# Batches 1 to 3 in chunks of 502 columns, and raw rows loaded by halves

## The chip, the cores and the metric

The kernel runs on one core of one Trainium2 chip. The metric is the device time of one execution in microseconds, from a median of runs. Engines: TensorE (PE, with its weight loads as PEld), VectorE (DVE), ScalarE (ACT), GpSimd (POOL) and SyncE (SP), which here only issues DMAs.

## The reference

```python
X = np.fft.fft(x, axis=1)              # x: (4, 3008, 256) f32, along 3008
X = np.fft.fft(X, axis=2)              # along 256
x = X.real.reshape(4 * 3008, 256)
h = x @ w_in                           # w_in: (256, 2048)
g = h * (1.0 / (1.0 + np.exp(-h)))
out = g @ w_out                        # w_out: (2048, 256)
```

## The kernel before

**The mathematics.** The transform along 256 is folded into w_in once, at the start (abh and abl, the high and low fp32r parts of the folded weights, and the row a128). The transform along 3008 is real-valued work on folded rows: sums and differences of four quarter-shifted and mirrored rows, then a product with cosine tables. By symmetry only 1506 columns of a batch are needed; each gives two outputs (signs + and -). They fall into four classes, CLASS, by the residue of the frequency: 376, 378, 376 and 376 columns. A class needs sums (sm) or rotated differences (ri) of the raw rows; operand(c) makes its operand xf from them, splits it into xh and xl, and transform(c) multiplies it with the tables into a PSUM pair. spread(c) turns that into uvh and uvl (high and low part, fp32r, ScalarE line 375 and VectorE line 378) and copies one row, which a DMA from SP (line 377) repeats on 128 partitions as ub.

**The main loop.** A chunk is one class of one batch: 16 chunks of 376 or 378 columns. Each has NF = 16 steps f, one for every 128 of the 2048 hidden columns. A step has four parts. first(c, f): 6 matmuls (lines 400 to 402, high x high, high x low, low x high, for two halves) into a pq pair in PSUM, of which there are two. act(c, f): VectorE adds ub times a128 (line 414) and makes sum and difference h (lines 418, 419), ScalarE applies Silu (430) and copies to gh (431). rest: VectorE makes gl = h - gh (441), one step later in its order. second(c, f): 12 matmuls (lines 458, 459, 465) into four accumulators in PSUM, LAG = 3 steps later. In chunk 0 twelve steps use f32 weights without the split (line 456), while w_out is converted. After f = 15 ScalarE copies the four accumulators to o tiles (473), four buffers shared with the row of spread, and SP writes them out (474).

**The order.** All is written out by hand. In the loop over steps come first(step), second(step - 3), at f = 12 the transform of the next class, act, rest(step - 1), spread of the transformed class, and then what plan holds for the step, and a few pieces of two queues: queue (operands, weight splits) with a budget of 0.6 a step and pool_queue (GpSimd's folds) with 0.6, in chunk 1 1.3. Each engine runs its own instructions in that order and waits on semaphores for the others.

**The folds.** load_x brings 4 x 2 x 256 raw values on 128 partitions (two buffers of 8 KB a partition), add_x adds the mirrored rows by an accumulating DMA from GpSimd's queue. fold_sums makes the sums and keeps the even-odd differences (od), fold_diffs reuses the same raw tile and od for the differences; ScalarE scales with the rotation (lines 254, 255) and GpSimd adds (259).

Of the kernel before, what the change touches and what calls it, by code (L numbers as in the profile page):

```python
# [50 lines left out]
def fft_mlp(ctx, tc, x1, x2, w_in, w_out, te, to, t2, t2f, rot1, rot2, dft, eye, out):  # L51
# [9 lines left out]
    cp = ctx.enter_context(tc.tile_pool(name="cp", bufs=2))  # L61
# [160 lines left out]
    def fold_diffs(k, i, ps=every):  # L222

        tt = nc.gpsimd.tensor_tensor
        g, od, rot = raw_x.pop((k, i))[ps], folded.pop(("od", k, i), None), rot_sb[k][ps]
        for h in range(2):
            if k + i == 0:
                tt(g[:, h, 0:2], g[:, h, 0:2], g[:, h, 2:4], op=ALU.subtract)
                yield 1.2
                keep = fold_p.tile([128, 2, 128], F32, tag="half", name="keep", bufs=3)[:, :, 1:]  # L230
                for j in range(2):
                    e, o = g[:, h, j, 1:128], g[:, h, j, 129:]
                    tt(keep[:, 1 - j], *((e, o) if j else (o, e)), op=ALU.subtract)
                yield 0.6
                tt(g[:, h, 0:2, 1:128], g[:, h, 0:2, 1:128], g[:, h, 0:2, 129:], op=ALU.add)
                nc.scalar.activation(g[:, h, 0:2, 129:], keep, AF.Copy)
                yield 0.6
                continue
            tt(g[:, h, 0:2, 0:129], g[:, h, 0:2, 0:129], g[:, h, 2:4, 0:129], op=ALU.subtract)
            yield 0.4  # L240
            if od:
                tt(g[:, h, 0, 129:], od[h][:, 1, 1:], od[h][:, 3, 1:], op=ALU.subtract)
                tt(g[:, h, 1, 129:], od[h][:, 2, 1:], od[h][:, 0, 1:], op=ALU.subtract)
            else:
                keep = fold_p.tile([128, 128], F32, tag="half", name="keep", bufs=3)[ps, 1:]
                tt(keep, g[:, h, 1, 129:], g[:, h, 3, 129:], op=ALU.subtract)
                tt(g[:, h, 1, 129:], g[:, h, 2, 129:], g[:, h, 0, 129:], op=ALU.subtract)
                nc.scalar.activation(g[:, h, 0, 129:], keep, AF.Copy)
            yield 0.6
        yield 0.6  # L250
        ri = fold_tile("ri", k, i, 2 - k)[ps]
        for h in range(2):
# [545 lines left out]
```

## Time and profile before

| | |
|---|---|
| time, median of 3 runs | 903.4 us (903.19 to 903.96) |
| profiled execution, span of its instructions | 901.8 us |
| TensorE busy | 881.9 us, 98%, 4982 matmuls |
| VectorE, ScalarE, GpSimd busy | 82%, 58%, 20% |
| chain that ended last | TensorE 92%, VectorE 4%, DMA 2% |

No time of its own is given for the profiled execution beside its span, so its own time is the span. Busy time counts the records of an engine; a matmul's record is longer than the time to the next one, since matmuls are pipelined, so starts and not durations tell TensorE's pace. In a row of the order of time the columns are start and length in us, engine, line, operation, out<-in, shapes and the number of merged instructions; a bracket holds the idle time before and what ended it.

### The profile page before, as it was taken

Reading aid. Unit: us, or ns where it says so; the run is one execution under the profiler, and the core shown is the slowest. Engines: PE = TensorE matmul, PEld = TensorE weight load, DVE = VectorE, ACT = ScalarE, POOL = GpSimd, SP = SyncE. Lnnn points to the kernel's source line nnn. Section 1 sums busy time; section 2 is a strip of 40 time slices with the busy share of each in tenths; the row PEclk is TensorE's granted clock in tenths of the full one; section 3 lists DMA queues with packets and bytes.
Section 4 is the critical chain, followed back from the end, with each engine's and each line's share of the span. In section 5 each row is a group of like instructions: output and inputs, shape, how many; then the busy total and the mean of one; then the engine's idle time right before and its main releaser. Section 6 shows DMA issues by size and latency. Waiting matters only on the chain.

```text
span 901.8 us, 12782 instructions
## 1 busy us (share of the span) xinstructions
PE 881.9 (98%) x4982; PEld 858.9 (95%) x4982; DVE 743.9 (82%) x1209; ACT 525.8 (58%) x728; POOL 179.4 (20%) x213
## 2 busy tenths in 40 slices
PE   6889999999999999999999999999999999999998
PEld 4567999999999999999999999999999999999998
DVE  6888888978889797987879698887879878786885
ACT  3625675646667564755746475665645656565554
POOL 1114051660123061460301025110100101010000
PEclk9999999999999999999999999999999999999999
DMA  9790315312030460203021060212103021210301
GB/s 297 159 300 8 44 24 79 82 5 39 1 29 17 71 159 4 41 1 25 20 10 35 3 134 1 10 35 9 35 2 42 1 9 35 9 35 1 44 1 35
DMA packets 19597, 42.65 MB, mean 47 GB/s; under 512 B 2464, under 2 KB 12704, under 8 KB 17616
## 3 DMA queue, kind: packets, MB, share of 16 engines
q1 hardware_dynamic: 17904, 31.87, 18.9%
q0 software_dynamic: 1632, 9.96, 5.5%
q8 instruction: 39, 0.64, 0.3%
q14 instruction: 22, 0.18, 0.1%
HBM read 26.39 MB, written 12.34 MB: 43 GB/s over the span
## 4 chain that ended last, share of the span: by engine, by line
PE 92%; DVE 4%; DMA 2%; issue 1%; ACT 1%; SPq 0%; DVEq 0%; ACTq 0%
PE acc L459 19%; PE acc L465 19%; PE acc L458 19%; PE pq L400 9%; PE pq L401 9%; PE pq L402 9%; PE pq L345 5%; DMA wo<-in_w_out_dram 1%; DMA win<-in_w_in_dram 1%; PE acc L456 1%; PE pq L210 1%; DVE wf L83 1%; PE pw L523 0%; DVE wf L85 0%; DVE wf L79 0%
## 5 line engine op out<-in xcount | busy, mean ns | idle before, releaser
L430 ACT ACTIVATE h<-h 128x752 f32<-128x752 f32 (+2 forms) x246 | 204.0, 829 | 284.3 <-DVE h L419 281.7
L459 PE MATMUL acc<-gh,wol 128*128 128x376 f32 (+1 forms) x976 | 326.8, 335 | 0.0
L458 PE MATMUL acc<-gh,woh 128*128 128x376 f32 (+1 forms) x976 | 326.3, 334 | 0.0
L441 DVE TENSOR_TENSOR gl<-h,gh 128x752 fp32r<-128x752 f32 (+2 forms) x246 | 242.0, 984 | 1.9 <-ACT gh L431 1.8
L465 PE MATMUL acc<-gl,woh 128*128 128x376 f32 (+1 forms) x976 | 216.1, 335 | 0.0
L431 ACT ACTIVATE gh<-h 128x752 fp32r<-128x752 f32 (+2 forms) x246 | 204.2, 830 | 7.8
L414 DVE SCALAR_TENSOR_TENSOR h<-ub,a,pq 128x376 f32<-128x376 f32 (+1 forms) x254 | 153.5, 604 | 58.3 <-PE pq L402 56.2
L459 PEld LDWEIGHTS acc<-gh,wol 128*128 128x128 f32 x976 | 183.7, 188 | 0.0
L458 PEld LDWEIGHTS acc<-gh,woh 128*128 128x128 f32 x976 | 183.5, 188 | 0.0
L400 PE MATMUL pq<-uvh,abh 128*128 128x376 f32 (+1 forms) x508 | 173.7, 342 | 2.8 <-DVE h L419 2.8
L465 PEld LDWEIGHTS acc<-gl,woh 128*128 128x128 f32 x976 | 172.8, 189 | 0.0
L401 PE MATMUL pq<-uvl,abh 128*128 128x376 f32 (+1 forms) x508 | 170.4, 335 | 0.0
L402 PE MATMUL pq<-uvh,abl 128*128 128x376 f32 (+1 forms) x508 | 170.2, 335 | 0.0
L419 DVE TENSOR_TENSOR h<-h,pq 128x376 f32<-128x376 f32 (+1 forms) x254 | 139.0, 547 | 8.7
L418 DVE TENSOR_TENSOR h<-h,pq 128x376 f32<-128x376 f32 (+1 forms) x254 | 138.9, 547 | 8.5
L320 POOL TENSOR_TENSOR xl<-xf,xh 128x256 fp32r<-128x256 f32 x53 | 49.6, 964 | 399.6 <-DVE h L419 244.6
L400 PEld LDWEIGHTS pq<-uvh,abh 128*128 128x128 f32 x508 | 95.6, 188 | 5.3 <-DVE h L419 4.0
L401 PEld LDWEIGHTS pq<-uvl,abh 128*128 128x128 f32 x508 | 95.9, 189 | 1.1
L402 PEld LDWEIGHTS pq<-uvh,abl 128*128 128x128 f32 x508 | 96.0, 189 | 0.0
L378 DVE TENSOR_TENSOR uvl<-pq,uvh 128x752 fp32r<-128x752 f32 (+1 forms) x16 | 15.1, 943 | 56.1 <-ACT row L376 56.1
L259 POOL TENSOR_TENSOR ri<-ri,raw 128x256 f32<-128x256 f32 (+1 forms) x28 | 27.5, 994 | 106.6 <-ACT ri L255 106.3
L456 PE MATMUL acc<-g,wof 128*128 128x376 f32 x96 | 33.5, 492 | 0.0
(117 smaller groups left out, 515.2 us busy)
## 6 DMA issues: line engine op xcount, KB each, us to landing
out_dram<-o SPq DMA_DIRECT2D x48, 188.0 KB, 2.3
raw<-in_x_dram SPq DMA_DIRECT2D x5, 1024.0 KB, 11.1
raw<-in_x_dram POOLq DMA_DIRECT2D x5, 1024.0 KB, 8.5
win<-in_w_in_dram SPq DMA_DIRECT2D x8, 512.0 KB, 9.4
wo<-in_w_out_dram SPq DMA_DIRECT2D x8, 512.0 KB, 9.9
out_dram<-o SPq DMA_DIRECT2D x16, 189.0 KB, 2.4
ub<-row SPq DMA_DIRECT2D x11, 188.0 KB, 8.7
te<-in_te_dram POOLq DMA_DIRECT2D x1, 1128.0 KB, 13.2
```

The lines of the kernel that those rows point to most:

```text
L400: nc.tensor.matmul(po, abh[:, i, fs], uvh[:, i, :n], start=True, stop=False)
L401: nc.tensor.matmul(po, abh[:, i, fs], uvl[:, i, :n], start=False, stop=False)
L402: nc.tensor.matmul(po, abl[:, i, fs], uvh[:, i, :n], start=False, stop=True)
L414: stt(p[:, :n], ub[:, :n], a128[f // 2][:, f % 2:f % 2 + 1], pq[:, 0, :n], op0=ALU.mult, op1=ALU.add)
L418: tt(h[:, 0, :n], p[:, :n], pq[:, 1, :n], op=ALU.add)
L419: tt(h[:, 1, :n], p[:, :n], pq[:, 1, :n], op=ALU.subtract)
L430: nc.scalar.activation(h[:, sg, :n], h[:, sg, :n], AF.Silu)
L431: nc.scalar.activation(gh[:, sg, :n], h[:, sg, :n], AF.Copy)
L441: tt(gl[:, sg, :n], g[:, sg, :n], gh[:, sg, :n].bitcast(F32), op=ALU.subtract)
L458: nc.tensor.matmul(po, wo[0][f // 2][:, f % 2, es], gh[:, sg, :n], start=f == 0, stop=False)
L459: nc.tensor.matmul(po, wo[1][f // 2][:, f % 2, es], gh[:, sg, :n], start=False, stop=False)
L465: nc.tensor.matmul(accs[c][i][:, :n], wo[0][f // 2][:, f % 2, es], gl[:, sg, :n], start=False, stop=f == NF - 1)
```

## The change

Batch 0 keeps four chunks, the class with k = 0 now first in the column order. The 4518 columns of batches 1 to 3 are cut into nine chunks of 502, without regard to classes, so a class can give columns to two chunks; spread writes each piece into its chunk. turns says at which step each class is transformed, begins when its operand is started. A raw tile now holds one half, and is loaded twice: for the sums and again for the differences, so od is gone, and both folds follow one plan (load, add 4 or 5 steps later, fold 3 steps after that). pool_queue's budget is 1.3 everywhere. h has two buffers instead of three, o three instead of four, uv and ub three. w_out's raw tiles use other buffers, the constants of the start share one tile with uv, and z is made in place in sm.

```diff
-CLASS = ((378, 376), (0, 378), (754, 376), (1130, 376))
-CH = 378
+CLASS = ((0, 376), (376, 378), (754, 376), (1130, 376))
+CH = 502
+CHUNKS = [n for _, n in CLASS] + [CH] * (3 * (B - 1))
+STARTS = [sum(CHUNKS[:j]) for j in range(len(CHUNKS))]
+LAST = len(CHUNKS) - 1
 LAG = 3
 FULL = 12
 DIRECT = 2
-PIECES = ((slice(0, 4),), (slice(0, 2), slice(2, 4)))
...
     def load_x(k, i, ps=every):
-        t = raw_x[k, i] = raws.tile([128, 2, 4, D], F32, tag="raw", name="raw")
-        nc.sync.dma_start(out=t[ps], in_=(x1, x2)[k][i, ps, 0])
+        for h in range(2):
+            t = raw_x[k, i, h] = raws.tile([128, 4, D], F32, tag="raw", name="raw")
+            nc.sync.dma_start(out=t[ps], in_=(x1, x2)[k][i, ps, 0, h])
 
     def add_x(k, i, ps=every):
 
-        nc.gpsimd.dma_start(out=raw_x[k, i][ps], in_=(x1, x2)[k][i, ps, 1], accum_op=ALU.add)
-
-    def fold_tile(name, k, i, bufs=1):
+        for h in range(2):
+            nc.gpsimd.dma_start(out=raw_x[k, i, h][ps], in_=(x1, x2)[k][i, ps, 1, h], accum_op=ALU.add)
...
-        g = raw_x[k, i][ps]
-        if k == 0:
-            od = fold_p.tile([128, 2, 4, 128], F32, tag="od", name="od")
-            od = [od[ps, h] for h in range(2)]
-        else:
-            od = [fold_p.tile([128, 4, 128], F32, tag="half", name="od", bufs=3)[ps] for h in range(2)]
-        folded["od", k, i] = od
         sm = fold_tile("sm", k, i)[ps]
         for h in range(2):
-            for js in PIECES[k]:
-                tt(od[h][:, js, 1:], g[:, h, js, 1:128], g[:, h, js, 129:], op=ALU.subtract)
-                yield 0.6
-                tt(g[:, h, js, 1:128], g[:, h, js, 1:128], g[:, h, js, 129:], op=ALU.add)
-                yield 0.6
-            tt(sm[:, h, :, 0:129], g[:, h, 0:2, 0:129], g[:, h, 2:4, 0:129], op=ALU.add)
+            g = raw_x.pop((k, i, h))[ps]
+            tt(g[:, 0:2], g[:, 0:2], g[:, 2:4], op=ALU.add)
+            yield 0.6
+            tt(sm[:, h, :, 1:128], g[:, 0:2, 1:128], g[:, 0:2, 129:], op=ALU.add)
             yield 0.4
-            tt(sm[:, h, :, 129:], od[h][:, 0:2, 1:], od[h][:, 2:4, 1:], op=ALU.add)
+            tt(sm[:, h, :, 129:], g[:, 0:2, 1:128], g[:, 0:2, 129:], op=ALU.subtract)
+            nc.scalar.activation(sm[:, h, :, ends], g[:, 0:2, ends], AF.Copy)
             yield 0.4
-
-    def first_sums(k, ps=every):
-
-        g = raw_x[k, 0][ps]
+        ready.add(("sm", k, i, ps.stop))
...
+    def chunk(j):
+        if j not in chunks:
+            uv = cp.tile([128, 2, 2, 512], F32R, tag="uv", name="uv")
+            chunks[j] = uv[:, 0], uv[:, 1], cp.tile([128, 512], F32, tag="ub", name="ub"), CHUNKS[j], STARTS[j]
+        return chunks[j]
+
     def spread(c, po):
 
-        uvh = cp.tile([128, 2, CH], F32R, tag="uvh", name="uvh")
-        uvl = cp.tile([128, 2, CH], F32R, tag="uvl", name="uvl")
-        ub = cp.tile([128, CH], F32, tag="ub", name="ub")
         b, k = divmod(c, 4)
         o, n = CLASS[k]
         o += b * NC
-        row = mp.tile([1, CH], F32, tag="o", name="row", bufs=4)
-        nc.scalar.activation(uvh[:, :, :n], po[:, :, :n], AF.Copy)
-        nc.scalar.activation(row[:, :n], po[0:1, 1, :n], AF.Copy)
-        (nc.sync if c else nc.gpsimd).dma_start(out=ub[:, :n], in_=row[:, :n].unsqueeze(0).to_broadcast([1, 128, n]))
-        tt(uvl[:, :, :n], po[:, :, :n], uvh[:, :, :n].bitcast(F32), op=ALU.subtract)
-        chunks[c] = uvh, uvl, ub, n, o
+        parts = []
+        for j, (at, m) in enumerate(zip(STARTS, CHUNKS)):
+            lo, hi = max(o, at), min(o + n, at + m)
+            if lo < hi:
+                uvh, uvl, ub, _, _ = chunk(j)
+                src, dst = slice(lo - o, hi - o), slice(lo - at, hi - at)
+                parts.append((uvh[:, :, dst], uvl[:, :, dst], ub[:, dst], src))
+        for uvh, _, _, src in parts:
+            nc.scalar.activation(uvh, po[:, :, src], AF.Copy)
+        for _, _, ub, src in parts:
+            row = mp.tile([1, CH], F32, tag="o", name="row", bufs=3)[:, :src.stop - src.start]
+            nc.scalar.activation(row, po[0:1, 1, src], AF.Copy)
+            (nc.sync if c else nc.gpsimd).dma_start(
+                out=ub, in_=row.unsqueeze(0).to_broadcast([1, 128, src.stop - src.start]))
+        for uvh, uvl, _, src in parts:
+            tt(uvl, po[:, :, src], uvh.bitcast(F32), op=ALU.subtract)
...
-            h = mp.tile([128, 2, CH], F32, tag="h", name="h", bufs=3)
+            h = mp.tile([128, 2, CH], F32, tag="h", name="h")
...
-                t = mp.tile([128, CH], F32, tag="o", name="o", bufs=4)
+                t = mp.tile([128, CH], F32, tag="o", name="o", bufs=3)
...
+    turns, begins = {}, {1: (0, 3), 2: (1, 9), 3: (2, 0), 4: (3, 2), 5: (3, 7), 6: (4, 0)}
+    for c in range(1, 4):
+        turns[c - 1, 12 + 2 * (c == 2)] = c
+    for b in range(1, B):
+        j, c = 3 * b + 1, 4 * b
+        for k, when in enumerate(((j - 1, 0 if b > 1 else 7), (j - 1, 12 if b > 1 else 14), (j, 8), (j + 1, 4))):
+            turns[when] = c + k
+            begins.setdefault(c + k + 1, when)
+        begins[c + 4], begins[c + 6] = (j + 1, 8), (j + 3, 3)
+    for c in range(1, 4 * B):
+        at(*begins[c], add, queue, ("op", c), operand(c))
...
+    def fold(name, k, i, j, f, *ps):
+        at(j, f, load_x, k, i, *ps)
+        at(j, f + 5 - (j < 3), add_x, k, i, *ps)
+        at(j, f + 8 - (j < 3), add, pool_queue, (name, k, i), {"sm": fold_sums, "ri": fold_diffs}[name](k, i, *ps))
+
+    at(0, 9, add, pool_queue, ("ri", 0, 0), fold_diffs(0, 0))
+    fold("ri", 1, 0, 0, 13)
+    fold("sm", 0, 1, 1, 9)
+    fold("sm", 1, 0, 2, 5, up)
+    fold("ri", 0, 1, 3, 1)
     for b in range(1, B - 1):
-        c = 4 * b + 1
-        at(c - 1, 14, load_x, 0, b + 1)
-        at(c, 0, add_x, 0, b + 1)
-        at(c, 4, add, pool_queue, ("t1", b + 1), fold_sums(0, b + 1))
-        at(c, 4, add, pool_queue, ("t1d", b + 1), fold_diffs(0, b + 1))
+        j = 3 * b + 1
+        fold("sm", 0, b + 1, j, 0)
+        fold("ri", 0, b + 1, j + 1, 6)
         if b % 2:
-            at(c - 1, 14, load_x, 1, b // 2 + 1)
-            at(c, 1, add_x, 1, b // 2 + 1)
-            at(c, 5, add, pool_queue, ("t2", b), fold_sums(1, b // 2 + 1))
-            at(c + 1, 5, add, pool_queue, ("t2d", b), fold_diffs(1, b // 2 + 1))
+            fold("sm", 1, b // 2 + 1, j, 11)
+            fold("ri", 1, b // 2 + 1, j + 2, 5)
...
-            if f == 12 and c + 1 < 4 * B:
+            turn = turns.get((c, f)) if n < len(steps) else None
+            if turn:
+                drain(queue, upto=("op", turn))
+                drain(pool_queue, upto=("x", turn))
                 new = pq_tile()
-                transform(c + 1, new)
+                transform(turn, new)
...
-            drain(pool_queue, 1.3 if c == 1 else 0.6)
+            drain(pool_queue, 1.3)
```

The new fold_diffs, which is not in this cut:

```python
def fold_diffs(k, i):
    tt = nc.gpsimd.tensor_tensor
    rot = rot_sb[k]
    for h in range(2):
        g = raw_x.pop((k, i, h))
        tt(g[:, 0:2], g[:, 0:2], g[:, 2:4], op=ALU.subtract)
        yield 0.6
        even, odd = g[:, 0:2, 1:128], g[:, 0:2, 129:]
        tt(g[:, 2:4, 1:128], even, odd, op=ALU.add)
        nc.scalar.activation(g[:, 2:4, ends], g[:, 0:2, ends], AF.Copy)
        yield 0.4
        tt(g[:, 2, 129:], even[:, 1], odd[:, 1], op=ALU.subtract)
        tt(g[:, 3, 129:], odd[:, 0], even[:, 0], op=ALU.subtract)
        yield 0.4
        ri = fold_tile("ri", k, i)
        for j in range(2):
            nc.scalar.activation(g[:, j], g[:, 3], AF.Copy, scale=rot[:, h, 1 - j:2 - j])
            nc.scalar.activation(ri[:, h, j], g[:, 2], AF.Copy, scale=rot[:, h, j:j + 1])
            yield 0.3
        for j, op in ((0, ALU.subtract), (1, ALU.add)):
            tt(ri[:, h, j], ri[:, h, j], g[:, j], op=op)
            yield 0.4
```

## Rows read from the trace of the kernel before

**Rows 1.** Busy time over the span: us, share, instructions.

```profile
PE 881.9 (98%) x4982; PEld 858.9 (95%) x4982; DVE 743.9 (82%) x1209; ACT 525.8 (58%) x728; POOL 179.4 (20%) x213
```

**Rows 2.** Waits of TensorE: us in total, times, longest.

```profile
PE pq L400 <- DVE h L419: 2.8, 2, 2.5
PE pq L334 <- DVE xf L272: 2.5, 1, 2.5
```

**Rows 3.** Stretch: PE, PEld, DVE, ACT, POOL busy, clock, DMA share, GB/s.

```profile
107.00:896.00 789.00, 789.00 (x4598) 789.00 (x4597) 658.53 (x1054) 474.45 (x643) 159.23 (x176) 1.00 0.20 31
```

**Rows 4.** Order of time on TensorE: one row a step, chunks 5 and 6.

```profile
323.93 0.85 PE L465 MATMUL acc<-gl,woh 128*128 128x378 f32 x4
...
352.05 0.85 PE L465 MATMUL acc<-gl,woh 128*128 128x378 f32 x4
...
376.97 0.85 PE L465 MATMUL acc<-gl,woh 128*128 128x376 f32 x4
...
401.84 0.85 PE L465 MATMUL acc<-gl,woh 128*128 128x376 f32 x4
```

**Rows 5.** Order of time on TensorE, f32 matmuls of the start.

```profile
16.37 3.60 PE L210 MATMUL pq<-raw,eye_sb 128*128 128x512 f32 x8
19.80 1.89 PE L523 MATMUL pw<-wf,dft_sb 128*128 128x256 f32 x8
21.53 1.02 PE L210 MATMUL pq<-minus,eye_sb 128*128 128x512 f32 x2
```

**Rows 6.** Instructions by line and form: busy us, mean ns, idle before.

```profile
L414 DVE SCALAR_TENSOR_TENSOR h<-ub,a,pq 128x376 f32<-128x376 f32 x190 | 114.7, 604 | 45.2 <-PE pq L402 43.7
L418 DVE TENSOR_TENSOR h<-h,pq 128x376 f32<-128x376 f32 x190 | 103.7, 546 | 6.3
L441 DVE TENSOR_TENSOR gl<-h,gh 128x752 fp32r<-128x752 f32 x178 | 173.3, 974 | 0.0
L430 ACT ACTIVATE h<-h 128x752 f32<-128x752 f32 x178 | 148.6, 835 | 212.6 <-DVE h L419 212.1
```

**Rows 7.** The tile ub: its row transfers, issue to landing.

```profile
DMA to landing us min/median/max: 8.6/8.7/9.1
```

**Rows 8.** DMA issues by tile: KB each, median us to landing.

```profile
out_dram<-o SPq DMA_DIRECT2D x48, 188.0 KB, 2.3
...
a<-rows POOLq DMA_DIRECT2D x8, 1.0 KB, 5.1
```

**Rows 9.** Order of time around the turn in chunk 2.

```profile
195.93 1.19 PE L345 MATMUL pq<-to,xl 128*128 128x376 f32 x6
196.96 0.34 PE L400 MATMUL pq<-uvh,abh 128*128 128x376 f32 x1
...
197.85 0.46 ACT L376 ACTIVATE row<-pq 1x376 f32<-1x376 f32 x1
198.34 0.48 SPq L377 DMA_DIRECT2D ub<-row  x1
...
207.51 0.61 DVE L414 SCALAR_TENSOR_TENSOR h<-ub,a,pq 128x376 f32<-128x376 f32 x1 [0.47 <-PE pq L402]
```

**Rows 10.** Order of time at the end: last copies and output DMAs.

```profile
896.20 2.04 ACT L473 ACTIVATE o<-acc 128x376 f32<-128x376 f32 x4 [3.48 <-PE acc L465]
...
896.72 2.11 SPq L474 DMA_DIRECT2D out_dram<-o  x4
```

**Rows 11.** Order of time in chunk 0: the end of TensorE's long wait.

```profile
66.61 0.44 PE L400 MATMUL pq<-uvh,abh 128*128 128x376 f32 x1 [2.49 <-DVE h L419]
```

**Rows 12.** Busy time by engine in three short stretches, columns as before.

```profile
27.70:31.00 3.30, 3.30 (x11) 2.04 (x12) 3.15 (x10) 1.24 (x3) 0.00 (x0) 1.00 0.97 342
67.20:70.60 3.40, 3.40 (x9) 2.31 (x8) 3.06 (x7) 2.64 (x4) 0.00 (x1) 0.50 0.23 85
...
76.00:80.00 4.00, 4.00 (x18) 2.98 (x18) 3.93 (x8) 0.00 (x0) 3.84 (x6) 1.00 0.00 0
```

More of the change, by code (lines that the diff above doesn't have):

```diff
@@ L208, in row_sums @@
             for j in range(2):
-                src = minus[h, j] if part else raw_x[0, 0][:, h, 2 * j:2 * j + 2]
+                src = minus[h, j] if part else raw_x[0, 0, h][:, 2 * j:2 * j + 2]
                 nc.tensor.matmul(po[:, h, :], eye_sb, src.rearrange("p j d -> p (j d)"),
@@ L220, in split_sums @@
         tt(sm[:, :, :, 129:], p[:, :, :, 1:128], sm[:, :, :, 129:], op=ALU.subtract)
-    def fold_diffs(k, i, ps=every):
+    def fold_diffs(k, i):
         tt = nc.gpsimd.tensor_tensor
-        g, od, rot = raw_x.pop((k, i))[ps], folded.pop(("od", k, i), None), rot_sb[k][ps]
+        rot = rot_sb[k]
         for h in range(2):
[L227 to L239, printed above, removed]
-            yield 0.4
[L241 to L252, printed above, removed]
@@ L258, in fold_diffs @@
             for j, op in ((0, ALU.subtract), (1, ALU.add)):
-                tt(ri[:, h, j], ri[:, h, j], g[:, h, 2 + j], op=op)
+                tt(ri[:, h, j], ri[:, h, j], g[:, j], op=op)
                 yield 0.4
+        ready.add(("ri", k, i, 128))
     operands = {}
@@ L267, in operand @@
         hs = slice(64 * (b % 2), 64 * (b % 2) + 64)
+        name = "sm" if k < 2 else "ri"
+        if b or k > 1:
+            assert (name, 0, b, 128) in ready, c
+            assert any((name, 1, b // 2, p) in ready for p in ((64, 128)[b % 2], 128)), c
         xf = xs.tile([128, 1280], F32, tag="xf", name="xf")
@@ L282, in operand @@
             sm, sm2 = folded["sm", 0, b], folded["sm", 1, b // 2]
-            z = (fold_p if b else tabs_p).tile([128, 2, 2, D], F32, tag="od", name="z")
-            tt(z[:, 0], sm[:, :, 0], sm[:, :, 1], op=ALU.add)
-            tt(z[hs, 1], sm2[hs, :, 0], sm2[hs, :, 1], op=ALU.add)
+            tt(sm[:, :, 0], sm[:, :, 0], sm[:, :, 1], op=ALU.add)
+            tt(sm2[hs, :, 0], sm2[hs, :, 0], sm2[hs, :, 1], op=ALU.add)
             l0 = xf[:, :768].rearrange("p (a d) -> p a d", a=2)
@@ L373, in spread @@
         o += b * NC
-        row = mp.tile([1, CH], F32, tag="o", name="row", bufs=4)
-        nc.scalar.activation(uvh[:, :, :n], po[:, :, :n], AF.Copy)
-        nc.scalar.activation(row[:, :n], po[0:1, 1, :n], AF.Copy)
-        (nc.sync if c else nc.gpsimd).dma_start(out=ub[:, :n], in_=row[:, :n].unsqueeze(0).to_broadcast([1, 128, n]))
-        tt(uvl[:, :, :n], po[:, :, :n], uvh[:, :, :n].bitcast(F32), op=ALU.subtract)
-        chunks[c] = uvh, uvl, ub, n, o
+        parts = []
[14 more added lines that the diff above has]
+            tt(uvl, po[:, :, src], uvh.bitcast(F32), op=ALU.subtract)
         if c == 0:
-            for p, uv in enumerate((uvh, uvl)):
-                nc.scalar.activation(vneg[:, p, :n], uv[:, 1, :n].bitcast(F32), AF.Copy, scale=turn[:, :])
+            for p, uv in enumerate(chunks[0][:2]):
+                nc.scalar.activation(vneg[:, p, :n], uv[:, 1, :n].bitcast(F32), AF.Copy, scale=flip[:, :])
     pqs, gs, accs = {}, {}, {}
@@ L403, in signs @@
     def signs(c, f):
-        return (slice(0, 1), slice(1, 2)) if c == 4 * B - 1 and f >= NF - 2 else (slice(0, 2),)
+        return (slice(0, 1), slice(1, 2)) if c == LAST and f >= NF - 2 else (slice(0, 2),)
     def act(c, f, fill=()):
@@ L502, in fft_mlp @@
     ps = late.enter_context(tc.tile_pool(name="ps", bufs=4, space=PSUM))
-    dft_sb = wr.tile([128, 2, 2, 128], F32, name="dft_sb")
-    eye_sb = wr.tile([128, 128], F32, name="eye_sb")
-    rows = wr.tile([128, 2, 128, 2], F32, name="rows")
+    once = cp.tile([128, 2048], F32, tag="uv", name="once")
+    dft_sb = once[:, 0:512].rearrange("p (c m k) -> p c m k", c=2, m=2)
+    rows = once[:, 512:1024].rearrange("p (q k t) -> p q k t", q=2, t=2)
+    eye_sb, zero, warm = once[:, 1024:1152], once[0:1, 1152:1408], once[0:1, 1408:1409]
+    x2_lo = cp.tile([128, 2, 4, D], F32, tag="uv", name="x2_lo")[lo]
     win, wf32, pws, conv = {}, {}, {}, {}
@@ L544, in fft_mlp @@
     nc.sync.dma_start(out=eye_sb, in_=eye)
-    load_x(1, 0, lo)
+    nc.sync.dma_start(out=x2_lo, in_=x2[0, lo, 0])
     load_w(2)
@@ L557, in fft_mlp @@
     nc.gpsimd.memset(zero, 0.0)
-    nc.gpsimd.memset(turn, -1.0)
-    nc.gpsimd.memset(turn[0:1], 1.0)
-    warm = wr.tile([1, 1], F32, name="warm")
+    nc.gpsimd.memset(flip, -1.0)
+    nc.gpsimd.memset(flip[0:1], 1.0)
     nc.scalar.activation(warm, zero[:, :1], AF.Silu)
-    add_x(1, 0, lo)
+    nc.gpsimd.dma_start(out=x2_lo, in_=x2[0, lo, 1], accum_op=ALU.add)
     nc.sync.dma_start(out=rot_sb[0], in_=rot1)
@@ L584, in fft_mlp @@
     row_sums(rs, 1)
-    run(first_sums(1, lo))
+    run(first_sums(1, x2_lo, lo))
     large(2)
@@ L610, in fft_mlp, with at @@
     large(6)
-    steps = [(c, f) for c in range(4 * B) for f in range(NF)]
+    steps = [(j, f) for j in range(len(CHUNKS)) for f in range(NF)]
     plan = {}
-    def at(c, f, fn, *a):
-        plan.setdefault((c, f), []).append((fn, a))
+    def at(j, f, fn, *a):
+        j, f = j + f // NF, f % NF
+        plan.setdefault((j, f), []).append((fn, a))
     def add(q, name, work):
         q.append((name, work))
-    for c in range(4 * B - 1):
-        at(c, {0: 3, 1: 8, 3: 6}.get(c, 0), add, queue, ("op", c + 1), operand(c + 1))
+    turns, begins = {}, {1: (0, 3), 2: (1, 9), 3: (2, 0), 4: (3, 2), 5: (3, 7), 6: (4, 0)}
@@ L685, in fft_mlp @@
         if new:
-            spread(c + 1, new)
+            spread(turn, new)
         if n < len(steps):
@@ L764, in _columns @@
     m = np.arange(376)
-    k = np.concatenate([8 * np.arange(190), 8 * np.arange(188) + 4, 4 * m + 2, 8 * m + 1, 8 * m + 5])
-    neg = np.concatenate([np.ones(378, bool), m % 2 == 1, np.zeros(752, bool)])
-    keep = np.arange(NC) != 189
+    k = np.concatenate([4 * m + 2, 8 * np.arange(190), 8 * np.arange(188) + 4, 8 * m + 1, 8 * m + 5])
+    neg = np.concatenate([m % 2 == 1, np.ones(378, bool), np.zeros(752, bool)])
+    keep = np.arange(NC) != 376 + 189
     k1 = np.where(neg, -k, k) % S
```

45 lines of the change are left out of this document (17 added, 28 removed).

## The prediction, as it was before the run

> **What bounds the kernel now.** I read the busy shares first. TensorE is busy for 98% of the span and VectorE for 82% [rows 1], but a mean share can hide a stage with another limit, so next come the waits of TensorE: beside those for the first products at the start it waits twice on VectorE's line 419, 2.8 us together, and once 2.5 us on line 272 [rows 2]. From 107 to 896 us TensorE is busy for 789.00 of 789.00 us at granted clock 1.00, while VectorE has 658.53 us of work there, ScalarE 474.45 and GpSimd 159.23 [rows 3]. So every step of the main part lasts as long as its 18 matmuls (6 of the first product, 12 of the second), and what the others do is hidden as long as they keep up. A busy share does not say how close TensorE is to its own best, so the third view is its order of time: when does the same matmul of the next step start?
>
> **Fewer, longer matmuls.** In a chunk of 378 columns nine steps take 352.05 - 323.93 = 28.12 us, 3.124 us each, 173.6 ns for each of 18 matmuls. In the chunk of 376 columns behind it eight steps take 401.84 - 376.97 = 24.87 us, 3.109 each, 172.7 ns [rows 4]. At the full clock of 2.4 GHz, one column in a cycle, 376 columns are 156.7 ns: 16.0 ns of each matmul are not columns. The change makes 9 chunks of 502 in batches 1 to 3 from 12 chunks of 376 or 378. The columns stay 1506 in a batch, but the matmuls in the steps go from 3 x 4 x 16 x 18 = 3456 to 2592, and what a matmul costs beside its columns is paid 864 times less.
>
> How does that rest grow with the length? From 376 to 378 columns a step grows by 15.6 ns, 0.43 ns a column and matmul [rows 4] (the rows are rounded to 0.01 us, so 0.37 to 0.50). 126 columns more are then 54.7 ns, and a matmul of 502 takes 227.4 ns, a step 4.093 us. Before: 3 x 16 x (3 x 3.109 + 3.124) = 597.6 us. After: 144 x 4.093 = 589.4 us. **Gain: 8.2 us.** The bounds are far apart. Below: the f32 matmuls at the start take (19.80 - 16.37) / 8 = 429 ns for 512 columns and (21.53 - 19.80) / 8 = 216 ns for 256, thus 0.83 ns a column in two passes and a rest of 4 ns [rows 5]; with that rest 502 columns take 213 ns, a step 3.834 us, and the gain is 45.5 us. Above: in proportion to the columns, 172.7 x 502 / 376 = 230.6 ns, a step of 4.150 us, 597.7 us, no gain. I take 227.4 because it comes from the same kind of matmul in neighbouring chunks; the f32 rows are another kind, with two passes for one weight load.
>
> Here the Trainium skill can be weighed. TensorE: Matmul & The Clock Gate, section Back-to-back issue gap, gives for a warm array N / 2.4 + 2.5 ns. The trace does not agree at 376 columns: 172.7 ns and not 159.2 [rows 4]. If only those 2.5 ns were paid per matmul, the change would save 864 x 2.5 = 2.2 us; that reading stands beside the first rival below.
>
> **Do the others keep up?** VectorE's four long instructions of a step take 604 + 546 + 547 + 974 = 2.67 us (line 419 costs what 418 does), ScalarE's two, lines 430 and 431, 835 each, 1.67 us [rows 6]. Even in full proportion to the columns that is 3.57 and 2.23 us against 4.093. The pieces of a class that go to two chunks add six pairs of small instructions to ScalarE and VectorE and six row transfers over the kernel; they lie in the same slack. The second load of x adds DMA work, but the queues are 20% busy in the main part [rows 3]. GpSimd loses the even-odd subtractions and worked 159 of 789 us. With two h buffers in place of three, line 414 of step n + 2 writes what line 441 of step n read, and VectorE has that behind it in its own order: nothing. The in-place z: nothing. Each load in halves costs SP one more issue; behind a load that waits for its raw buffer, SP holds the row and output transfers, but between two loads there are at least eleven steps (over 34 us), far more than GpSimd's work on a pair of halves. The first differences move from chunk 1 into chunk 0, where VectorE already worked 3.93 of 4.00 us beside a busy GpSimd [rows 12]: the same company, so 0, between -1 and +1.5 us.
>
> **The row transfer at chunk 2.** The bias row of a class goes to 128 partitions by a DMA that lands 8.6 to 9.1 us after its issue, median 8.7 [rows 7]. Before, the transform stands in step 12, three steps ahead of the next chunk. In chunk 2 the first matmul after it starts at t = 196.96, the row is copied at 197.85 for 0.46 us, the DMA issued at 198.34 = t + 1.4, so it lands at t + 10.1; line 414 of the next chunk starts at 207.51 = t + 10.55 [rows 9]. There is 0.5 us to spare. The change puts the transform of class 2 in step 14 of chunk 1, two steps (6.2 us) later against its use: line 414 is wanted at t + 4.3 and gets its row at t + 10.1. VectorE waits 5.8 us, and behind the waiting instruction stand line 441 of the step before and the next steps' sums. TensorE runs on for the steps for which it has PSUM: the third step after t would start at t + 3 x 3.109 = t + 9.3, but its pq buffer is read until t + 10.1 + 0.60 + 0.55 + 0.55 = t + 11.8. **Cost: 2.5 us**; 0 if the row should come as early as an output transfer, which lands in 2.3 us [rows 8].
>
> Class 5 is put late too, in step 14 of chunk 3, but its first piece is 126 columns. Needed by line 414 so that TensorE isn't held: issue at t + 1.5, landing L, 2.3 us of VectorE, all by t + 3.11 + 2 x (6 x 0.227 + 12 x 0.173) = t + 10.0, so L up to 6.2 us. A transfer of 128 pieces of 8 bytes lands in 5.1 us [rows 8], the full row in 8.7; by columns between these, 6.3. Cost 0; at 8.7 it is 2.5. The skill's page DMA: Bandwidth & Descriptors, Specifications, puts the full rate at pieces of 512 B and more; these are 504 B. By it the late end and the 2.5 us would be the likelier; no row here has such a piece, and I leave it in the range.
>
> All other turns leave three steps or more, of 4.09 us each in the later batches.
>
> **The end.** The last class's four copies start at 896.20, the first output DMA, 0.52 us after its copy began, at 896.72 [rows 10]; it lands 2.3 us later [rows 8]. With three o buffers the fourth copy waits for that landing. After: copies follow the accumulators, 3 x 0.227 = 0.68 us apart, the first DMA goes out some 0.65 us after its copy begins and lands at 0.65 + 2.3 to 3.1 (in proportion to bytes) = 2.95 to 3.7, where the fourth could have started at 2.05: 0.9 to 1.7 us, and the last transfer takes up to 0.8 longer. **Cost: 1.5 us** (0.9 to 2.5). At the other chunk ends the same wait holds ScalarE some 1.2 us; what it then makes late, gh, is used by TensorE three steps on.
>
> **Sum.** The span of 901.8 us becomes 901.8 - 8.2 + 2.5 + 1.5 = 897.6 us. The median of the runs, 903.4, is 1.6 us above the span; with the same 1.6 the forecast is 899.2 us.
>
> **Rivals.** *All in proportion.* The rest of 16 ns is not a fee but a lower rate of columns, 0.459 ns each in place of 0.417. For it: the measured 0.43 lies between the two, and its rounding reaches to 0.50. Against it: 0.43 is nearer to 0.417. Place: each matmul of batches 1 to 3. Gain 0, the costs stay: 903.4 + 0.1 + 4.0 = 907.5 us, slower. It decides from 229.0 ns a matmul on, where 2592 x 229.0 = 597.6 - 4.0. *The rest shrinks with length,* as in the f32 rows: 213 ns, 903.4 - 45.5 + 4.0 = 861.9 us. Against it: going from 376 to 378 the rest did not shrink. *More held than I count.* After TensorE's wait of 2.49 us in chunk 0, which ended at 66.61 [rows 11], the granted clock was 0.50 from 67.2 to 70.6 us, which costs half of 3.4, 1.7 us; after the equal wait on line 272 it stayed at 1.00 [rows 2, 12]. If the wait at chunk 2 is followed by that, or class 5's piece is late too, or ScalarE, whose scaled copies stand in program order behind GpSimd's differences, is held up in chunks 1 to 3: 901 to 905 us.
>
> **Chances.** Forecast 0.58, with its own range 893.5 (0.417 ns a column, gain 13.9) to 902; proportion 0.17; shrinking rest 0.07; more held 0.18. A measurement of this kernel tells 0.2% (1.8 us) from no change: faster is below 901.6, slower above 905.2. Faster: 0.49 of the forecast's, the 0.07 and a quarter of the 0.18, 0.60. Slower: the proportion's nearly whole 0.17 and some of the 0.18, 0.22. Same: 0.18. The range runs from 891 to 907: the shrinking rest and the upper half of the proportion stay outside.
>
> **What would show it.** The start-to-start time of line 465 in the new chunks: 4.09 us a step (4.05 by 0.417 ns, 4.15 in proportion, 3.83 with the shrinking rest). A wait of line 414 on the row DMA of some 6 us at the first step of chunk 2, and a wait of TensorE's line 400 of 2.5 us two steps later, with or without half the clock after it. Four copies at the end with a gap of 0.9 to 1.7 us before the last. Wrong it would be if TensorE showed waits in the batches of 502 columns, or if a step there were longer than its matmuls.

## The result and the profile after

The changed kernel takes 916.1 us (median, 915.0 to 916.99) against 903.7 us for the kernel before on the same chip: ratio 1.0141, 95% interval 1.0127 to 1.0155. It is slower, and the forecast of 899.2 us was wrong in sign. The profiled execution after spans 915.2 us, before 901.8.

Busy time of the page after, which answers to [rows 1]:

```profile
PE 881.5 (96%) x4118; PEld 751.8 (82%) x4118; DVE 718.9 (79%) x1023; ACT 504.2 (55%) x642; POOL 173.2 (19%) x211
```

864 matmuls are gone, and TensorE is busy for the same time. Its busy share of 96% hides what happened, because a matmul's record is longer than the time to the next one (in a chunk of 502, 0.39 us against 0.23). So I added up, for every matmul of both traces, the time to the start of the next one less the ordinary time of its form (227.7 ns for 502 columns, 172.7 for 376, 173.5 for 378). The excess is TensorE's lost time.

| us | before | after |
|---|---|---|
| first matmul | 7.8 | 7.7 |
| ordinary matmuls | 876.1 | 868.7 |
| lost before 90 us | 13.5 | 13.1 |
| lost after 90 us | 0 | 20.6 |
| last matmul's start to the end | 4.4 | 5.1 |
| span | 901.8 | 915.2 |

The matmuls became 7.4 us cheaper, nearly as forecast; 20.6 us of new waits came at seven places: 1.6 us at 111, 5.4 at 160 to 171, 0.7 at 250, 4.7 at 269 to 276, 1.9 at 426, 4.4 at 498 to 505 and 2.0 at 642. Before there was none [rows 3]. Waits of TensorE after (engine, line, for whom, us in total, times, longest), which answer to [rows 2]:

```profile
PE acc L456 <- ACT o L471: 7.5, 6, 2.6
PE pq L398 <- DVE h L417: 5.9, 6, 2.4
PE pq L398 <- DVE uv L377: 2.9, 1, 2.9
```

The three lines hold three causes (of the second, 2.4 us are chunk 2's and 3.2 us lie before 90 us). The first is new in kind: TensorE waits for ScalarE's copy of an accumulator. The longest case, at a chunk's end, in order of time:

```profile
491.40 0.88 POOL L161 DMA_DIRECT2D raw<-in_x_dram  x1
491.49 0.33 SPq L156 DMA_DIRECT2D raw<-in_x_dram  x1
493.61 1.97 ACT L471 ACTIVATE o<-acc 128x502 f32<-128x502 f32 x3 [0.46 <-PE acc L463]
494.22 7.03 SPq L472 DMA_DIRECT2D out_dram<-o  x4
496.84 0.86 POOL L161 DMA_DIRECT2D raw<-in_x_dram  x1 [4.56 <-DMA raw<-in_x_dram]
500.30 0.59 ACT L471 ACTIVATE o<-acc 128x502 f32<-128x502 f32 x1 [4.73 <-DMA out_dram<-o]
500.95 0.50 PE L456 MATMUL acc<-gh,woh 128*128 128x502 f32 x1 [2.61 <-ACT o L471]
```

Three copies run, the fourth needs a fourth o buffer and waits for the first output transfer, which was issued at 494.22 and lands at 500.2: 6.0 us, beside a raw load and accumulating adds of 512 KB issued from 491.40 on. The next chunk's first product into the fourth accumulator can't start before that copy.

A slow landing is not the only way to this wait. At 426 and 642 us the transfers land in 2.1 us, and TensorE still waits 1.2 and 1.1 us, because ScalarE comes late to the copies, behind its scaled copies for the differences (lines 236, 237):

```profile
425.26 0.49 ACT L237 ACTIVATE ri<-raw,rot_sb 128x256 f32<-128x256 f32 x1
425.67 1.52 ACT L471 ACTIVATE o<-acc 128x502 f32<-128x502 f32 x3
429.14 0.49 PE L456 MATMUL acc<-gh,woh 128*128 128x502 f32 x1 [1.18 <-ACT o L471]
```

At the ends where neither happens (351, 567, 710, 778 and 847 us) ScalarE waits 0.8 us for the landing and TensorE not at all.

The second cause is chunk 2's row:

```profile
151.98 0.46 ACT L373 ACTIVATE row<-pq 1x376 f32<-1x376 f32 x1
152.47 0.48 SPq L374 DMA_DIRECT2D ub<-row  x1
...
161.10 0.61 DVE L412 SCALAR_TENSOR_TENSOR h<-ub,a,pq 128x376 f32<-128x376 f32 x1 [4.81 <-DMA ub<-row]
162.93 0.44 PE L398 MATMUL pq<-uv,abh 128*128 128x376 f32 x1 [2.36 <-DVE h L417]
```

The third stands at the end of chunk 3, at the turn of class 5:

```profile
262.92 1.29 POOL L225 TENSOR_TENSOR raw<-raw 128x512 f32<-128x512 f32 x1
264.24 0.21 ACT L229 ACTIVATE raw<-raw 128x4 f32<-128x4 f32 x1 [1.05 <-POOL raw L225]
265.63 0.50 PE L330 MATMUL pq<-to,xl 128*128 128x188 f32 x3
266.05 0.45 POOL L232 TENSOR_TENSOR raw<-raw 128x127 f32<-128x127 f32 x1
266.54 0.51 ACT L236 ACTIVATE raw<-raw,rot_sb 128x256 f32<-128x256 f32 x1 [2.09 <-POOL raw L232]
269.74 0.84 ACT L370 ACTIVATE uv<-pq 128x252 fp32r<-128x252 f32 x2
271.01 1.01 DVE L377 TENSOR_TENSOR uv<-pq,uv 128x252 fp32r<-128x252 f32 x2 [5.93 <-ACT row L373]
272.17 0.46 PE L398 MATMUL pq<-uv,abh 128*128 128x502 f32 x1 [2.94 <-DVE uv L377]
```

The transform is done at 266.1. ScalarE stands at lines 229 and 236, waiting for GpSimd's differences of batch 1, and takes uv only at 269.74; VectorE's line 377 reads the transform's pq pair until 272.0, and TensorE needs that pair.

Three of the waits were followed by a low clock (columns as in [rows 3], clock third from the end), with TensorE's time taken up by slower matmuls. The clock has two levels, 1.2 and 2.4 GHz; 0.55 and 0.57 are stretches that reach a little into the upper one:

```profile
163.90:167.40 3.50, 3.50 (x14) 3.50 (x13) 3.42 (x8) 2.06 (x4) 0.00 (x0) 0.55 0.00 0
272.40:275.80 3.40, 3.40 (x12) 3.00 (x12) 2.55 (x5) 1.66 (x2) 0.00 (x0) 0.57 0.79 28
501.60:505.00 3.40, 3.40 (x10) 2.71 (x9) 1.87 (x3) 3.23 (x4) 0.00 (x0) 0.50 0.54 143
```

At about half the clock, a stretch of 3.4 us does some 1.6 us of work less than at full, so about 5 of the 20.6 us are clock and not waiting.

### The profile page after: what moved, and what is told of

Read it like the earlier page. It is cut to its first block, busy times and chain, and to the rows that moved or that the text cites. A ratio compares the mean times of both kernels' runs of the same rounds, so it can differ in the third digit from the quotient of the medians.

```text
span 915.2 us, 10977 instructions
## 1 busy us (share of the span) xinstructions
PE 881.5 (96%) x4118; PEld 751.8 (82%) x4118; DVE 718.9 (79%) x1023; ACT 504.2 (55%) x642; POOL 173.2 (19%) x211
## 4 chain that ended last, share of the span: by engine, by line
PE 85%; DVE 5%; DMA 4%; ACT 3%; issue 2%; POOL 1%; SPq 0%; ACTq 0%; DVEq 0%
PE acc L463 17%; PE acc L456 17%; PE acc L457 16%; PE pq L398 9%; PE pq L399 9%; PE pq L400 9%; PE pq L330 5%; PE acc L454 2%; DMA out_dram<-o 2%; DMA ub<-row 1%; DMA win<-in_w_in_dram 1%; PE pw L523 1%; DVE h L412 1%; PE pq L207 1%; DVE h L416 1%
## 5 line engine op out<-in xcount | busy, mean ns | idle before, releaser
L428 ACT ACTIVATE h<-h 128x1004 f32<-128x1004 f32 (+3 forms) x198 | 194.1, 980 | 299.3 <-DVE h L417 296.3
L456 PE MATMUL acc<-gh,woh 128*128 128x502 f32 (+2 forms) x784 | 296.3, 378 | 7.6 <-ACT o L471 7.5
L457 PE MATMUL acc<-gh,wol 128*128 128x502 f32 (+2 forms) x784 | 295.0, 376 | 0.0
L439 DVE TENSOR_TENSOR gl<-h,gh 128x1004 fp32r<-128x1004 f32 (+3 forms) x198 | 234.5, 1185 | 6.8 <-ACT gh L429 6.8
L463 PE MATMUL acc<-gl,woh 128*128 128x502 f32 (+2 forms) x784 | 206.4, 377 | 0.0
L429 ACT ACTIVATE gh<-h 128x1004 fp32r<-128x1004 f32 (+3 forms) x198 | 194.3, 981 | 6.3
L398 PE MATMUL pq<-uv,abh 128*128 128x502 f32 (+2 forms) x412 | 157.7, 383 | 8.8 <-DVE h L417 5.9
L399 PE MATMUL pq<-uv,abh 128*128 128x502 f32 (+2 forms) x412 | 154.6, 375 | 0.0
L400 PE MATMUL pq<-uv,abl 128*128 128x502 f32 (+2 forms) x412 | 154.5, 375 | 0.0
L417 DVE TENSOR_TENSOR h<-h,pq 128x502 f32<-128x502 f32 (+2 forms) x206 | 131.5, 639 | 7.1
L416 DVE TENSOR_TENSOR h<-h,pq 128x502 f32<-128x502 f32 (+2 forms) x206 | 131.4, 638 | 6.8
L398 PEld LDWEIGHTS pq<-uv,abh 128*128 128x128 f32 x412 | 77.9, 189 | 23.9 <-DVE h L417 9.1
L399 PEld LDWEIGHTS pq<-uv,abh 128*128 128x128 f32 x412 | 77.8, 189 | 12.4
## 6 DMA issues: line engine op xcount, KB each, us to landing
wo<-in_w_out_dram SPq DMA_DIRECT2D x8, 512.0 KB, 10.6
```

Of the source, the lines that this page charges most:

```text
L398: nc.tensor.matmul(po, abh[:, i, fs], uvh[:, i, :n], start=True, stop=False)
L399: nc.tensor.matmul(po, abh[:, i, fs], uvl[:, i, :n], start=False, stop=False)
L400: nc.tensor.matmul(po, abl[:, i, fs], uvh[:, i, :n], start=False, stop=True)
L416: tt(h[:, 0, :n], p[:, :n], pq[:, 1, :n], op=ALU.add)
L417: tt(h[:, 1, :n], p[:, :n], pq[:, 1, :n], op=ALU.subtract)
L428: nc.scalar.activation(h[:, sg, :n], h[:, sg, :n], AF.Silu)
```

## The experiments

Two theories went in. A: the waits are separate, and each goes with its own cause (o buffers, class 2's late turn, class 5's turn). The rival: the second load and the differences leave too little time in chunks 1 to 3, so that a wait taken away comes back elsewhere. Times are medians, ratios stand to the kernel before on the same chip.

**Four o buffers**

```diff
-            row = mp.tile([1, CH], F32, tag="o", name="row", bufs=3)[...]
+            row = mp.tile([1, CH], F32, tag="o", name="row", bufs=4)[...]
-                t = mp.tile([128, CH], F32, tag="o", name="o", bufs=3)
+                t = mp.tile([128, CH], F32, tag="o", name="o", bufs=4)
```

> The changed kernel with four o buffers again instead of three, nothing else. Theory A (the fourth output copy waits for the landing of the first output DMA, ScalarE holds the accumulator, TensorE waits): TensorE's waits at the chunk ends go (1.57 + 1.12 + 1.34 + 2.77 + 1.26 us of lost time, and 1.66 us of the half clock after the longest), and some 0.9 us at the end: 916.1 - 10.6 = 905.5 us. Theory B (the second load of x makes transfers late, and whatever waits for them waits anyway): at most 3 us less, 913 or more. Theory C (TensorE only arrives earlier at the next wait): about half, 910.

907.7 us, ratio 1.0034 (1.0022 to 1.0046): 8.4 us of the 12.4 come back. TensorE's waits on line 471 fall from 7.5 to 0.4 us; nothing is lost at 498 any more, though the output transfers there still take up to 6.4 us. In the profiled executions the loss after 90 us falls from 20.6 to 10.3 us and the end gets 0.6 us shorter, 10.9 us, as theory A said (10.6); the start of this one lost 1.5 us more. The buffer is the largest cause.

**Class 2's turn two steps earlier**

```diff
-        turns[c - 1, 12 + 2 * (c == 2)] = c
+        turns[c - 1, 12] = c
```

> The changed kernel with the transform of class 2 in step 12 of chunk 1 instead of step 14. Theory A (the bias row of that class needs 8.7 us to land and is issued too late by two steps): the wait of VectorE on the row DMA (4.81 us) and of TensorE (2.5 us) at the first steps of chunk 2 goes, and with it 1.7 us of half clock: 911.9 us. Rival (the operand of class 2 isn't ready by step 12, so the transform itself holds TensorE): 915 or more, with a wait of line 330 on GpSimd or ScalarE.

917.7 us, 1.0147 (1.0125 to 1.0168): no gain. The loss at 160 fell only from 5.4 to 3.1 us, and 0.7 us came up at the earlier turn, which waits for GpSimd's xl. The row, issued earlier, took 12.0 us; VectorE still waits 2.8 us for it. TensorE's own wait behind it fell to 0.2 us and the low clock went, but ScalarE comes late to the copies of the accumulators, and with three o buffers TensorE waits 0.9 and 1.2 us for those (line 471).

**Class 5's turn two steps earlier**

```diff
-... (j - 1, 12 if b > 1 else 14) ...
+... (j - 1, 12) ...
```

> The changed kernel with the transform of class 5 in step 12 of chunk 3 instead of step 14. Theory A (the copies of its result, uv, stand on ScalarE behind copies that wait for GpSimd's differences, and two steps are too few to hide that): TensorE's wait of 3.1 us at the first step of chunk 4 and 1.7 us of half clock go: 911.3 us. Rival (ScalarE is held by GpSimd in the steps before just as long, so the copies come as late as now, or the fold now stands ahead of something else): 914 to 917.

919.7 us, 1.0167 (1.0152 to 1.0181): slower by 3.6. Here theory A fell. The loss at 250 to 268 grew from 5.4 (0.7 + 4.7) to 7.4 us:

```profile
255.91 1.26 ACT L298 ACTIVATE xh<-xf 128x1280 fp32r<-128x1280 f32 x1
257.25 4.64 POOL L305 TENSOR_TENSOR xl<-xf,xh 128x256 fp32r<-128x256 f32 x5 [11.80 <-ACT xh L298]
...
261.25 0.35 PE L330 MATMUL pq<-te,xl 128*128 128x190 f32 x1 [2.40 <-POOL xl L305]
```

The earlier turn finds its operand unfinished, and the transform itself waits. Of the 2.0 us that came on top, 1.7 are clock: it stays at 0.50 for 6.8 us after this wait, and for 3.4 in the changed kernel.

**All three edits together**

> The three edits together: four o buffers, class 2 and class 5 in step 12. Theory A (three separate causes, and a pace of 227.6 ns a matmul of 502 columns that is already there): 916.1 - 10.6 - 4.2 - 4.8 = 896.5 us, under the kernel before (903.7) by what the longer matmuls give less 0.6. Theory B (traffic): 908 or more. Theory C (waits that move): 900 to 906.

907.0 us, 1.0029 (1.002 to 1.0038): by the median the buffer's gain and no more. In the trace the loss at chunk 2 falls to 1.9 us (4.0 with four buffers alone), and that at class 5's turn rises from 5.5 to 7.1 as in the last run. Class 2's row was issued at 147.00, well in time, and still landed late:

```profile
144.72 1.76 POOL L161 DMA_DIRECT2D raw<-in_x_dram  x2
...
147.00 0.48 SPq L374 DMA_DIRECT2D ub<-row  x1
...
158.64 0.61 DVE L412 SCALAR_TENSOR_TENSOR h<-ub,a,pq 128x376 f32<-128x376 f32 x1 [2.69 <-DMA ub<-row]
```

It took 11.5 us, not 8.7 [rows 7], with two adds of 512 KB issued just before it. So the turns' rows, the row loads and the differences are tied together, and a turn has to be moved with the operand and the loads around it. The next three do that.

**Four buffers, both turns earlier, with their operands and loads**

```diff
-... {1: (0, 3), 2: (1, 9), 3: (2, 0), 4: (3, 2), 5: (3, 7), 6: (4, 0)}
+... {1: (0, 3), 2: (1, 8), 3: (2, 0), 4: (3, 0), 5: (3, 5), 6: (4, 0)}
-        turns[c - 1, 12 + 2 * (c == 2)] = c
+        turns[c - 1, 12] = c
-... ((j - 1, 0 if b > 1 else 7), (j - 1, 12 if b > 1 else 14), ...
+... ((j - 1, 0 if b > 1 else 5), (j - 1, 12), ...
-    fold("ri", 1, 0, 0, 13)
-    fold("sm", 0, 1, 1, 9)
+    fold("ri", 1, 0, 0, 12)
+    fold("sm", 0, 1, 1, 13)
```

> Four o buffers; class 2's turn at step 12 of chunk 1, with its operand begun one step earlier, and the second half of batch 1's rows loaded four steps later, so that its adds no longer lie beside class 2's row; operands 4 and 5 begun at steps 0 and 5 of chunk 3 and their turns at 5 and 12, ahead of the differences of batch 1. Theory A (separate waits, each gone when its own cause is gone; nominal matmuls and tail 881.0 us of span, start 3.5 + 2.8 to 4.5 + 6.7): span 895 to 897, median 896 to 898, ratio 0.991 to 0.994. Theory B (the second load and the differences on GpSimd keep the path short of time wherever they fall, so the waits move): waits of 3 to 7 us come up at other places before 300 us, median 901 to 907.

901.8 us, 0.9977 (0.9968 to 0.9986): within theory B's range, but without its new waits of 3 to 7 us. The loss at chunk 2 is gone, and its row, with those adds moved away, lands in 8.7 us; which of the edits did it (turn, operand, loads) this run does not split. What is left stands where it stood, at the end of chunk 3, 4.1 us:

```profile
255.72 0.84 ACT L370 ACTIVATE uv<-pq 128x252 fp32r<-128x252 f32 x2
256.99 1.01 DVE L377 TENSOR_TENSOR uv<-pq,uv 128x252 fp32r<-128x252 f32 x2 [1.48 <-ACT row L373]
258.14 0.65 PE L398 MATMUL pq<-uv,abh 128*128 128x376 f32 x1 [2.31 <-ACT ri L237]
```

The profile names line 237 as releaser, but line 377 is the one that ends just before, at 258.00, and it reads the pq pair that TensorE needs. The differences of batch 1 still hold ScalarE at this turn.

**Of these edits, only those of classes 4 and 5, with four buffers**

> Four o buffers, and only operands 4 and 5 and their turns earlier (steps 0 and 5 begin, 5 and 12 turn), class 2 left as in the changed kernel. Theory A: of the 907.7 us with four buffers the 4.7 us before chunk 4 go, 903.0; the 3.9 us at the start of chunk 2 stay. Theory B: the loss before chunk 4 stays at 4 to 7 us, 907 to 910.

905.8 us, 1.0024 (1.0014 to 1.0034), between the two: the loss at the end of chunk 3 is 2.5 us in place of 4.7, the one at chunk 2 stays at 4.1. Most of the 2.2 us is a low clock that did not come after this wait, which itself fell only from 2.9 to 2.3 us. By the medians class 2's edits are worth the 4.1 us between this kernel and the last; in the two traces the losses after 90 us are 8.1 and 5.4.

**The fifth kernel, and the differences of batch 1 four steps later**

```diff
-    fold("ri", 0, 1, 3, 1)
+    fold("ri", 0, 1, 3, 5)
-... 5: (3, 5), 6: (4, 0)}
+... 5: (3, 5), 6: (4, 4)}
```

> The fifth experiment's kernel, with the differences of batch 1 (their loads, adds and GpSimd's work) four steps later, so that class 5's turn at step 12 of chunk 3 lies ahead of them, and operand 6 begun at step 4 of chunk 4, after them. Theory A (what is left, 0.5 and 4.1 us at 239 to 261 us, is ScalarE behind GpSimd's differences at class 5's turn, so that TensorE waits for a buffer that the uv copies hold, with the half clock after it): both go, span 894.8 to 895.5, median 896.5 to 898, ratio 0.992 to 0.994; after 90 us TensorE then loses about 1 us in all, as the kernel before (0), and what is left of the change is the pace. Theory B (the wait moves again): 2 to 5 us are lost at class 6's turn, at 285 to 300 us, median 900 to 903.

897.9 us, 0.9934 (0.992 to 0.9947): faster than both kernels, as theory A said. After 90 us TensorE loses 1.6 us in all. Busy time by engine in its main part:

```profile
90.00:890.00 800.00, 799.23 (x3821) 693.88 (x3821) 647.52 (x890) 461.61 (x567) 152.25 (x169) 1.00 0.25 43
```

So the second load, the halves, the two h buffers and the other parts of the change that this kernel keeps cost no more than this once each wait is scheduled away; that they leave too little time is refuted for this plan, and true only of the plan of the changed kernel.

**Three buffers, the next batch's loads three steps later**

```diff
-        fold("sm", 0, b + 1, j, 0)
+        fold("sm", 0, b + 1, j, 3)
```

> The changed kernel with its three o buffers, where the loads of the next batch's rows for the sums go out three steps later (step 3 of the chunk, not 0), and their adds and folds with them. Theory A (the long wait of 4.4 us at 498 us is the output transfers held up beside those loads): that end loses 0.7 to 2.0 us like the other ends, median 912.5 to 914. Theory C (three buffers alone make the wait, loads or not): no change there, 916.

914.9 us, 1.0125 (1.0112 to 1.0139). In the trace the loss at 498 is gone altogether, more than expected:

```profile
496.92 3.21 SPq L472 DMA_DIRECT2D out_dram<-o  x4
499.18 0.59 ACT L471 ACTIVATE o<-acc 128x502 f32<-128x502 f32 x1 [0.91 <-DMA out_dram<-o]
500.23 0.86 SPq L156 DMA_DIRECT2D raw<-in_x_dram  x2
```

The transfer lands in 2.2 us with the loads behind it. The median gained only 1.2 us. In the profiled executions the loss after 90 us falls by 4.3 us, but this one's first matmul came 1.0 us later and it lost 1.5 us more before 90 us, where it ran 3.4 us at half the clock; the edit touches neither. The long wait is the meeting of outputs and loads, as the trace shows; the median alone would not prove it.

**The kernel before with three o buffers**

The same two numbers as in the first experiment, 4 to 3, in the old kernel.

> The kernel before with three o buffers in place of four, nothing else. Theory A (the fourth copy of a chunk waits for the first output transfer whatever the chunk's width): 15 chunk ends that lose 0 to 2 us, 5 to 8 us in all, median 909 to 912. Theory D (only the longer chunks with their larger transfers and second load run into it): within 1.5 us of 903.7.

920.0 us, 1.018 (1.0166 to 1.0194): 16.2 us slower, far above what both theories gave. TensorE loses 17.1 us after 90 us at nine places, 8.8 of them at one chunk end:

```profile
322.39 0.87 POOL L158 DMA_DIRECT2D raw<-in_x_dram  x1 [1.86 <-DVE h L419]
323.58 1.52 ACT L473 ACTIVATE o<-acc 128x376 f32<-128x376 f32 x3
324.10 10.60 SPq L474 DMA_DIRECT2D out_dram<-o  x4
333.85 0.48 ACT L473 ACTIVATE o<-acc 128x376 f32<-128x376 f32 x1 [8.74 <-DMA out_dram<-o]
334.38 0.68 PE L458 MATMUL acc<-gh,woh 128*128 128x378 f32 x1 [7.21 <-ACT o L473]
```

The old kernel had the same meeting of outputs with accumulating adds from GpSimd's queue, two of 1024 KB each. Its landing times (min, median, max) of line 474, and below them those of line 472 after:

```profile
DMA to landing us min/median/max: 1.9/2.3/9.6
```

```profile
DMA to landing us min/median/max: 1.9/2.1/6.3
```

With four buffers nothing waits for them. With three, narrow chunks take 920.0 us and wide ones 916.1; with four, 903.7 and 907.7.

## Why the prediction was wrong

**Fewer, longer matmuls: right.** Same line and view as [rows 4], two of the starts in a chunk of 502, seven steps apart:

```profile
530.79 1.08 PE L463 MATMUL acc<-gl,woh 128*128 128x502 f32 x4
...
559.50 1.07 PE L463 MATMUL acc<-gl,woh 128*128 128x502 f32 x4
```

28.71 / 7 = 4.10 us a step, 227.9 ns a matmul; forecast 4.093 and 227.4. The ordinary matmuls fell by 7.4 us in place of 8.2. In proportion (4.15) and the shrinking rest (3.83) are both out. That the f32 rows behind the latter are "two passes" was read off their 0.83 ns a column; no run shows passes apart. The Trainium skill, TensorE: Matmul & The Clock Gate, Back-to-back issue gap, has N / 2.4 + 2.5 ns for an isolated warm matmul, 211.7 ns here; 227.9 was measured, so the trace does not bear it out at 502 columns either.

**The o buffers at the other chunk ends: the step that failed.** It said that the wait "holds ScalarE some 1.2 us" and that "what it then makes late, gh, is used by TensorE three steps on". Two things were wrong. The wait also holds the accumulator: each of the four has one PSUM buffer, the fourth is free only after the late copy, and the next chunk writes it after 12 matmuls, 2.7 us, not three steps later. And 1.2 us was worked out with the median landing of 2.3 us [rows 8] and copies that begin on time. That holds at five ends, where nothing was lost; the loss came where the landing was slow (up to 6.3 us after, 9.6 before) and where ScalarE began its copies late. The cost was 8.4 us by the medians of the first experiment. I took the price of a lost buffer from a row that groups 48 transfers, and did not look at their spread, at what shares the queues at each end, or at what stands before the copies on ScalarE. The Trainium skill, DMA: Bandwidth & Descriptors, Issuing engines are not separate DMA queues, says that DMAs of SyncE and GpSimd interleave on the same engines; the output transfers at 494.22, slow beside loads and adds and 2.2 us without them, agree with it.

**The end: mechanism right, smaller.** The fourth copy waits 0.78 us, forecast 0.9 to 1.7:

```profile
908.51 1.95 ACT L471 ACTIVATE o<-acc 128x502 f32<-128x502 f32 x3 [4.96 <-PE acc L463]
909.13 3.06 SPq L472 DMA_DIRECT2D out_dram<-o  x4
911.24 0.59 ACT L471 ACTIVATE o<-acc 128x502 f32<-128x502 f32 x1 [0.78 <-DMA out_dram<-o]
```

From the last matmul to the end it cost 0.7 us, not 1.5.

**Chunk 2's row: right in mechanism and wait, too small in sum.** VectorE waits 4.81 us (forecast 5.8) and TensorE 2.36 (2.5). But the low clock behind it (0.55) and a wait of 1.0 us for a copy of o bring the loss there to 5.4 us; the sum had 2.5.

**Class 5's late turn: costed at 0, measured 4.7 us.** The row was faster than estimated. Six pieces of 126 columns land in 6.3 us by their median, the value that I had put between the bounds, but none of them took that: three, issued first of a pair, landed in 4.5 us and three, issued behind another piece, in 8.1 to 8.3. The view of the six, and below it that of class 5's piece alone:

```profile
ub<-row SPq DMA_DIRECT2D x6, 63.0 KB, 6.3
```

```profile
DMA to landing us min/median/max: 4.5/4.5/4.5
```

Being 504 B long did not make it late: the pieces of 1000 B, issued first of a pair too, took 6.8 us. What came late was uv, behind ScalarE's scaled copies for the differences. I had followed the row alone through this turn, not all that spread issues. The last rival names this very hold-up of ScalarE, and the clock; its bound of 905 us lacked the buffers. That it was one of the cases and not a term is why the sum fell on the wrong side.

**In one line.** 916.1 us is 897.9 with next to nothing in the way (the forecast without its 4.0 us of waits and end: 895.2), 8.4 for the o buffer and 9.9 for chunk 2, class 5 and the differences: 1.9, 4.1 and 3.9 us as they were taken away in turn. The two that were taken in other orders (class 2 or class 5 alone, with three buffers) gave nothing, so these shares hold in that order only, and since the low clock came after some of these waits and not after others, each can be off by the 1.6 us that it costs. The losses of 0.4 to 0.6 us that remain at three places were not pursued.

## What to carry to other kernels

When a buffer is taken away, follow what its last user frees, and price the wait place by place: by the landing where the transfer meets other loads, not by the median, and by when the copies themselves can begin. When a step is moved, follow each thing it issues: its operand, its copies on an in-order engine, its row, and the transfers that run beside it. An engine that is busy without a gap can be made faster only if all that it waits for still comes in time at the new pace; here 7.4 us of gain were real from the first run and were seen only when nearly all the waits were gone.

## What was not expected of the hardware

A wait of the same length was followed by a low clock in one run and not in another. At the same turn, before TensorE's line 398, the fifth experiment's kernel (class 2 moved too) waited 2.31 us and ran at 0.56 of the clock after it (columns as above):

```profile
258.60:262.00 3.40, 3.40 (x13) 3.40 (x13) 3.19 (x6) 1.93 (x3) 1.01 (x2) 0.56 0.78 30
```

The one without class 2's edits waited 2.30 us there and kept the full clock:

```profile
263.13 0.42 PE L398 MATMUL pq<-uv,abh 128*128 128x376 f32 x1 [2.30 <-ACT ri L237]
```

```profile
264.00:268.00 4.00, 4.00 (x25) 4.00 (x24) 3.79 (x7) 2.25 (x3) 0.66 (x1) 1.00 0.81 30
```

As with the two equal waits of [rows 2, 11, 12], the length of a wait did not decide it. Nor did the program alone: of four executions of the changed kernel two had a mean granted clock of 0.994 and took 916.9 and 917.0 us, and two had 0.997 and 0.998 and took 915.3 and 915.0. What did stays open.
